# Sign bits of the weights on VectorE or GpSimd, the schedule choosing per piece, in an attention and feed-forward kernel

## The chip, the core and the metric

The kernel runs on one core of a Trainium2 chip. Its engines work side by side, each on its own in-order queue of instructions: TensorE (PE, with weight loads as PEld), VectorE (DVE), ScalarE (ACT), GpSimd (POOL) and SyncE (SP, which here only issues transfers). The metric is the device time of one execution in microseconds, lower is better. A chance or a change is called "faster" or "slower" below only beyond 0.2%.

## The reference

Sliding-window attention with sinks over 4 batches of 8 heads, 768 positions, 64 wide, followed by a feed-forward layer with ELU on the 3072 tokens:

```python
scores = scale * np.matmul(q, k.transpose(0, 1, 3, 2))
keep = is_sink | in_window          # 4 sinks, window 128
a = softmax(np.where(keep, scores, -1e9))
x = (a @ v).transpose(0, 2, 1, 3).reshape(3072, 512)
h = x @ w_in                         # 512 -> 2048
g = np.where(h > 0.0, h, np.exp(np.minimum(h, 0.0)) - 1.0)
out = (g @ w_out).astype(np.float32) # 2048 -> 512
```

The weights `w_in` and `w_out` are 64-bit floats, so each number reaches the chip as two 32-bit words.

## The kernel before

The 24 tiles of 128 tokens are worked in nine chunks of two or three tiles (`SIZES`). A chunk runs through attention (scores, L614 in the first four chunks and L607/L608 later; the masked minimum, L633; the exponential, L635; division and rounding to two 16-bit halves, L685 and L686; a transposing DMA, L704; values, L670 in the first chunk and L718/L723 later) and then through 16 feed-forward steps f. A step is twelve matmuls into `h` (L782), the ELU on ACT, DVE and POOL (L790, L792, L793), rounding to the halves `gh` (L795, ACT) and `gl` (L796, POOL), and matmuls into `acc` (L803). The first two chunks are interleaved: chunk 0 does steps 0 to 6, chunk 1 steps 0 to 12, then both are finished (`PARTS`).

The weights come once, in 32 pieces of 128x512 numbers; piece 2f is for L782 of step f and piece 2f+1 for L803. Piece k is loaded as 128x1024 words into one of six `raw` buffers and rebuilt as a 32-bit float by `weight_f32`: ACT scales the upper word (L308, into a PSUM bank), DVE takes the three top bits of the lower word (L309) and the sign (L310), each into one 16-bit half of the buffer `wu` (two buffers), and DVE joins the three (L311, into `wv`). Then ACT rounds it to 16 bits (L460) and POOL makes the remainder in two halves of 256 columns (L461), both into the tiles `w`. In the rows of the order the tiles `w_135` to `w_166` are pieces 0 to 31, `raw_129` to `raw_134` the six buffers, and `wu_127` and `wu_128` the two.

The order on each queue is not written out. `Plan` is a list scheduler: every task has an engine, a duration, a latency and its dependences; `backward` gives due times from the places of the matmul tasks, `forward` starts the task that is due first among those that are ready, with a lock that makes POOL work and some DVE work (`slow` over 1) exclude each other. A task with `or_` may go to a second engine, whichever picks it first. It is repeated eight times and the best plan is kept (`order`); `keep_order` then emits the instructions in the order of their planned starts. So a change of one task's ways can move any instruction on any queue.

Of the kernel before, what the change touches and what calls it, by code (L numbers as in the profile page):

```python
# [9 lines left out]
F32 = mybir.dt.float32  # L10
F32R = mybir.dt.float32r
F16 = mybir.dt.float16
BF16 = mybir.dt.bfloat16
# [3 lines left out]
ALU = mybir.AluOpType  # L17
# [39 lines left out]
RINGS = dict(tp=2, tp_=2, kqs=2, kq=3, vs=2, vm=1, vt=6, sk=2, e=3, st=6, pq=3, pt=6, g=2, gh=3, x=7, wv=4, s=2, po=1, h=2, wu=2, sv=2, wps=1, raw=6)  # L57
# [44 lines left out]
class Plan:  # L102
# [7 lines left out]
    def add(self, eng, dur, fn, *args, deps=(), lat=0.0, pos=None, or_=None, line=0, slow=1.0, lock=True):  # L110

        t = Task(eng, dur, fn, args, deps, lat, pos, slow)
        t.line = line
        t.lock = lock
        if or_:
            t.ways[or_[0]] = or_[1:]
        self.tasks.append(t)
        return t

    def ring(self, name, writers, users):  # L120

        r = self.rings.setdefault(name, [])
        r.append((writers, users))
# [158 lines left out]
def act_us(n, scaled=False):  # L282
    return 0.17 + 0.00088 * n + (0.08 if scaled else 0.0)
# [6 lines left out]
def pool_us(n):  # L290
    return 0.18 + 0.0019 * n


def dma_us(nbytes):
    return nbytes / 330e3
# [4 lines left out]
def weight_f32(nc, v, d, u, raw):  # L300

    ui = u.bitcast(U16).rearrange("p (f t) -> p f t", t=2)
    words = raw.rearrange("p (f t) -> p f t", t=2)
    halves = raw.bitcast(U16).rearrange("p (f t) -> p f t", t=4)
    return (
        lambda: nc.scalar.activation(d, words[:, :, 1].bitcast(F32), AF.Copy, scale=2.0**-111),  # L308
        lambda: nc.vector.tensor_scalar(ui[:, :, 0], halves[:, :, 1], 13, None, ALU.logical_shift_right),  # L309
        lambda: nc.vector.tensor_scalar(ui[:, :, 1], halves[:, :, 3], 0x8000, None, ALU.bitwise_and),  # L310
        lambda: nc.vector.scalar_tensor_tensor(v.bitcast(I32), d.bitcast(I32), 3, u, ALU.logical_shift_left, ALU.bitwise_or),  # L311
    )
# [49 lines left out]
def fast_path(tc, ctx, first, kq, vx, wt, out, low, spread, numbers, flag):  # L362

    nc = tc.nc
# [4 lines left out]
    def rows(name, shape, dtype, n=None, mem=pool):  # L369
        return [mem.tile(shape, dtype, name=f"{name}{i}") for i in range(n or RINGS[name])]  # L370
# [21 lines left out]
    wu = rows("wu", [P, 512], I32)  # L392
# [18 lines left out]
    add, ring = plan.add, plan.ring  # L411
    turn = {}

    def slot(name):
        turn[name] = turn.get(name, -1) + 1
        return turn[name] % RINGS[name]
# [17 lines left out]
    def weights(k):  # L434
        raw, v = raws[slot("raw")], wv[slot("wv")]

        def load():
            if wide:
                nc.sync.dma_start(raw, wt[k].bitcast(I32))
            else:  # L440
                nc.sync.dma_start(raw[:, :512].bitcast(F32), wt[k])

        def step(i):
            return lambda: weight_f32(nc, v, acc[2], wu[k % RINGS["wu"]], raw)[i]()

        ld = add("SP", 0.4, load, deps=[w_done.get(k - AHEAD, [None])[0]], lat=1.45)
        if wide:
            a = add("ACT", act_us(512), step(0), deps=[ld])
            u1 = add("DVE", 0.446, step(1), deps=[ld], slow=2.0)
            u2 = add("DVE", 0.446, step(2), deps=[ld], slow=2.0)  # L450
            b = add("DVE", 0.7, step(3), deps=[a, u1, u2])
            ring("wu", [u1, u2], [b])
            ring("wps", [a], [b])
            ring("raw", [ld], [a, u1, u2])
            first_acc2.append(b)
        else:
            a = b = add("ACT", act_us(512), lambda: nc.scalar.activation(v, raw[:, :512].bitcast(F32), AF.Copy, scale=W_SCALE), deps=[ld])
            ring("raw", [ld], [a])

        th = add("ACT", act_us(512), lambda: nc.scalar.activation(w[k][:, 0, :], v, AF.Copy), deps=[b])  # L460
        tls = [add("POOL", pool_us(256), lambda c=c: nc.gpsimd.tensor_tensor(w[k][:, 1, c], v[:, c], w[k][:, 0, c], ALU.subtract), deps=[th]) for c in (slice(0, 256), slice(256, 512))]  # L461
        tl = tls[-1]
        ring("wv", [b], tls)
        w_done[k] = th, *tls

    for k in range(NW):
        weights(k)
# [384 lines left out]
    for c, ch in enumerate(CHUNKS):  # L852
        t, n = vm[slot("vm")], len(ch) * P
        src = vx[:, ch[0] * VT : (ch[-1] + 1) * VT].rearrange("p (g w) -> p g w", g=len(ch))
        ld = add("SP", 0.4, lambda t=t, n=n, src=src: nc.sync.dma_start(t.rearrange("p a w -> p (a w)")[:, : NP * n].rearrange("p (g w) -> p g w", w=VT), src), deps=[exps_done[NF * 4 + 8 * c]], lat=dma_us(P * NP * n * 4))
# [293 lines left out]
```

## Time and profile before

| | us |
|---|---|
| median of 3 runs (641.25 to 641.39) | 641.27 |
| the profiled execution, whole | 641.34 |
| its span in the trace | 639.4 |
| PE busy | 613.2 (96%) |
| DVE busy | 424.7 (66%) |
| ACT busy | 423.2 (66%) |
| POOL busy | 361.1 (56%) |

The 1.9 us between the span and the whole lie outside of the trace. The shares of busy time are averages over a start, in which the weights and the first chunks are prepared, and a long stretch after it; they have to be read stretch by stretch. The line numbers are those of the kernel before; behind L452 the changed kernel stands two lines lower, so that its L463 is L461 of before, and its L452 is the new instruction.

### The profile page before, as it was taken

What the parts mean: (1) busy time and instruction counts of PE and PEld (TensorE: products, weight loads), DVE (VectorE), ACT (ScalarE), POOL (GpSimd) and SP (SyncE); (2) the same over time, 40 slices, a digit from 0 to 9 for tenths busy, and PEclk for the clock granted to TensorE, in tenths of its full rate; (3) what the DMA queues carried; (4) which work ended last, traced back from release to release, by engine and by line L of the source; (5) the groups of instructions that cost most, each with busy time, mean ns of one, the idle gap of its engine ahead of it and who ended that gap; (6) DMA issues with size and microseconds to landing.
All of it is one profiled execution on the core that took longest, in us unless ns stands there. A gap on an engine that the chain in (4) does not pass through costs nothing.

```text
span 639.4 us, 13262 instructions
## 1 busy us (share of the span) xinstructions
PE 613.2 (96%) x4475; PEld 366.3 (57%) x4475; DVE 424.7 (66%) x1160; ACT 423.2 (66%) x1216; POOL 361.1 (56%) x630
## 2 busy tenths in 40 slices
PE   5977899999999999999999999999999999999996
PEld 4644565666666555555565655655555556555552
DVE  6998899877666865566666777568567866432222
ACT  5888788877777876676767776677666776432221
POOL 3587799764346766656546667556455664323221
PEclk9978999999999999999999999999999999999999
DMA  8597767467354874365537845446636634210001
GB/s 292 153 315 221 205 254 239 129 178 184 79 121 111 184 156 106 78 206 116 103 96 138 199 100 147 97 159 111 148 76 140 169 87 106 57 45 36 1 2 52
DMA packets 117660, 86.23 MB, mean 135 GB/s; under 512 B 97492, under 2 KB 97492, under 8 KB 117588
## 3 DMA queue, kind: packets, MB, share of 16 engines
q1 hardware_dynamic: 117588, 85.34, 52.3%
q8 instruction: 36, 0.59, 0.4%
q14 instruction: 36, 0.29, 0.2%
HBM read 54.39 MB, written 7.34 MB: 97 GB/s over the span
## 4 chain that ended last, share of the span: by engine, by line
PE 87%; POOL 3%; ACT 3%; DMA 2%; DVE 2%; issue 1%; SPq 0%; POOLq 0%; ACTq 0%; DVEq 0%
PE h L782 38%; PE acc L803 37%; PE po L718 4%; PE s L607 2%; PE s L608 2%; PE s L614 2%; POOL w L461 1%; PE acc L653 1%; DMA kqs<-in_kq_dram 1%; ACT e L635 1%; DMA vs<-in_vx_dram 1%; DMA pt<-pq 1%; ACT pq L685 1%; POOL gl L796 1%; PE po L723 0%
## 5 line engine op out<-in xcount | busy, mean ns | idle before, releaser
L782 PE MATMUL h<-x,w 128*128 128x384 f16 (+1 forms) x1728 | 277.6, 310 | 6.6 <-POOL w L461 3.5
L782 PEld LDWEIGHTS <-w 128*128 128x128 f16 x1728 | 165.2, 98 | 102.9 <-POOL w L461 5.6
L796 POOL TENSOR_TENSOR gl<-g,gh 128x384 f16<-128x384 f32 (+1 forms) x144 | 126.9, 882 | 133.5 <-ACT gh L795 100.1
L803 PE MATMUL acc<-w,gh 128*128 128x512 f16 x768 | 193.2, 381 | 0.0
L790 ACT ACTIVATE g<-h 128x384 f32<-128x384 f32 (+1 forms) x144 | 65.4, 454 | 106.6 <-PE h L782 93.5
L686 DVE SCALAR_TENSOR_TENSOR pq<-e,st,pq 128x256 f16<-128x256 f32 (+1 forms) x176 | 103.2, 618 | 14.4 <-ACT pq L685 14.2
L803 PEld LDWEIGHTS <-gh 128*128 128x128 f16 x768 | 71.0, 98 | 71.6 <-ACT g L790 1.7
L803 PE MATMUL acc<-w,gl 128*128 128x512 f16 x384 | 109.2, 379 | 0.1
L635 ACT ACTIVATE e<-e,st 128x264 f32<-128x264 f32 (+1 forms) x192 | 93.2, 486 | 15.9 <-DVE st L633 14.3
L792 DVE TENSOR_SCALAR g<-g 128x384 f32<-128x384 f32 (+1 forms) x76 | 37.5, 494 | 98.4 <-ACT g L790 98.1
L633 DVE CUSTOM_DVE_ANT_0 e<-s,m 128x264 f32<-128x264 f32 (+1 forms) x192 | 71.6, 404 | 44.1 <-PE s L608 35.9
L795 ACT ACTIVATE gh<-g 128x384 f16<-128x384 f32 (+1 forms) x144 | 69.6, 483 | 34.9 <-DVE g L793 33.2
L685 ACT ACTIVATE pq<-e,st 128x256 f16<-128x256 f32 (+1 forms) x176 | 78.2, 484 | 12.3 <-DVE st L640 6.4
L793 DVE SCALAR_TENSOR_TENSOR g<-g,h 128x384 f32<-128x384 f32 (+1 forms) x144 | 72.6, 504 | 20.0 <-POOL g L792 18.8
L803 PEld LDWEIGHTS <-gl 128*128 128x128 f16 x384 | 37.6, 98 | 45.9 <-POOL gl L796 0.6
L533 POOL TENSOR_TENSOR kq<-kqs,kq 128x528 fp32r<-128x528 f32 (+1 forms) x40 | 49.2, 1231 | 23.6 <-ACT kq L529 23.0
L792 POOL TENSOR_SCALAR g<-g 128x384 f32<-128x384 f32 (+1 forms) x68 | 34.5, 508 | 40.7 <-ACT g L790 34.1
L461 POOL TENSOR_TENSOR w<-wv,w 128x256 f16<-128x256 f32 x64 | 48.5, 774 | 6.2 <-ACT w L460 5.8
L529 ACT ACTIVATE kq<-kqs 128x912 fp32r<-128x912 f32 (+1 forms) x40 | 36.4, 913 | 14.8 <-PE s L608 12.1
L535 POOL TENSOR_TENSOR kq<-kqs,kq 64x384 fp32r<-64x384 f32 x40 | 41.1, 1026 | 3.1
L607 PE MATMUL s<-kq 128*128 128x264 f32 (+1 forms) x120 | 41.3, 365 | 0.0
L718 PE MATMUL po<-pt,vh 128*64 128x128 f16 x656 | 36.4, 223 | 1.7 <-DMA pt<-pq 1.6
(90 smaller groups left out, 642.3 us busy)
## 6 DMA issues: line engine op xcount, KB each, us to landing
raw<-in_wt_dram SPq DMA_DIRECT2D x32, 512.0 KB, 5.3
kqs<-in_kq_dram SPq DMA_DIRECT2D x24, 456.0 KB, 3.9
kqs<-in_kq_dram SPq DMA_DIRECT2D x20, 390.0 KB, 3.4
vs<-in_vx_dram SPq DMA_DIRECT2D x28, 256.0 KB, 3.5
out_dram<-wv SPq DMA_DIRECT2D x24, 256.0 KB, 3.7
vm<-in_vx_dram SPq DMA_DIRECT2D x6, 768.0 KB, 4.7
kqs<-in_kq_dram SPq DMA_DIRECT2D x8, 326.0 KB, 4.2
vm<-in_vx_dram SPq DMA_DIRECT2D x3, 512.0 KB, 4.2
```

The lines of the kernel that those rows point to most:

```text
L633: red = add("DVE", 0.24 + 0.001 * wd, lambda ee=ee, me=me, sp=sps[e], m=m, wd=wd: nc.vector.tensor_tensor_reduce(ee, sp[:, :wd], m[:, :wd] ...
L635: ex = add("ACT", 0.47 + 0.00085 * wd, lambda ee=ee, me=me, rs=rs[:, e : e + 1]: nc.scalar.activation(ee, ee, AF.Exp, bias=me, scale=-1.0, ...
L685: a = add("ACT", act_us(nb * P, True), lambda src=src, hi=hi, re=re: nc.scalar.activation(hi, src, AF.Copy, scale=re), deps=[rr])
L686: b = add("DVE", 0.478 if nb == 2 else 0.33, lambda src=src, hi=hi, lo=lo, re=re: nc.vector.scalar_tensor_tensor(lo, src, re, hi, ALU.mult ...
L718: nc.tensor.matmul(po[e * D : (e + 1) * D, oc], vts[i][x][:, vo : vo + D], pt[:, (2 * e + part) * nb + i, :], start=new, stop=last)
L782: nc.tensor.matmul(hp[:, :n], win[:, part, d, :], xx[:, :n], start=k == 0, stop=k == 3 * ND - 1)
L790: a = add("ACT", act_us(n) + 0.18, lambda gf=gf, hp=hp, sums=sums: nc.scalar.activation(gf, hp[:, :n], AF.Exp, scale=1.0 / G_SCALE, accum_ ...
L792: b = add("DVE", 0.14 + 0.00057 * n, lambda gf=gf: nc.vector.tensor_scalar(gf, gf, -1.0, G_SCALE, ALU.add, ALU.mult), deps=[a], slow=2.1, ...
L793: b = add("DVE", dve_us(n), lambda gf=gf, hp=hp: nc.vector.scalar_tensor_tensor(gf, gf, 0.0, hp[:, :n], ALU.min, ALU.max), deps=[b])
L795: th = add("ACT", act_us(n), lambda gf=gf, gh=gh: nc.scalar.activation(gh[:, :n], gf, AF.Copy), deps=[b])
L796: tl = add("POOL", pool_us(n), lambda gl=gl, gf=gf, gh=gh: nc.gpsimd.tensor_tensor(gl[:, :n], gf, gh[:, :n], ALU.subtract), deps=[th])
L803: nc.tensor.matmul(acc[i], gg[:, i * P : (i + 1) * P], wout[:, part, :], start=f == f0 and k == 0, stop=f == f1 - 1 and k == 2)
```

## The change

In `weights`, the task of the sign bits gets a second way. On DVE it is still L310: a 16-bit AND of the top quarter of the 64-bit number with 0x8000. On POOL it is one `tensor_scalar`: the upper word, read as a 32-bit float with a step of two words, times 0.0, written as bfloat16 into every second 16-bit place; the product is a zero that has the sign of the number, and a bfloat16 zero with sign is the same bits. The task also depends on the task of L309 in the plan. The price that the planner is given for POOL is 0.70 us, against 0.446 us (with `slow` 2.0) on DVE.

```diff
             u1 = add("DVE", 0.446, step(1), deps=[ld], slow=2.0)
-            u2 = add("DVE", 0.446, step(2), deps=[ld], slow=2.0)
+            sign = wu[k % RINGS["wu"]].bitcast(BF16).rearrange("p (f t) -> p f t", t=2)[:, :, 1]
+            high = raw.rearrange("p (f t) -> p f t", t=2)[:, :, 1].bitcast(F32)
+            u2 = add("DVE", 0.446, step(2), deps=[ld, u1], slow=2.0, or_=("POOL", 0.2 + 0.00098 * 512, lambda sign=sign, high=high: nc.gpsimd.tensor_scalar(sign, high, 0.0, None, ALU.mult)))
             b = add("DVE", 0.7, step(3), deps=[a, u1, u2])
```

Of the 32 pieces, 21 have their sign on POOL in the changed kernel: pieces 0 to 10, 12 and 13, and of the last eighteen 15, 16, 21, 24, 26, 28, 29 and 31. Behind that the plan is another one on every engine. Three places follow.

The first is DVE's queue between the masked minima of two tiles of chunk 1 (the tile with `st_98` and the next with `st_99`). Before:

```order
L633 ISA e_95,st_98<-s_170,m_181 128x264
L633 ISA st_98 128x1
L309 TENSOR_SCALAR wu_127<-raw_129 128x512
L310 TENSOR_SCALAR wu_127<-raw_129 128x512
L562 SCALAR_TENSOR_TENSOR vl_85<-vs_64,vh_79 128x512
L311 SCALAR_TENSOR_TENSOR wv_125<-acc_174,wu_127 128x512
L686 SCALAR_TENSOR_TENSOR pq_105<-e_96,st_102,pq_105 128x256 x2
L562 SCALAR_TENSOR_TENSOR vl_86<-vs_63,vh_80 128x512
L633 ISA e_96,st_99<-s_169,m_181 128x264
```

and now:

```order
L635 ISA e_95,st_98<-s_170,m_181 128x264
L635 ISA st_98 128x1
L688 SCALAR_TENSOR_TENSOR pq_105<-e_96,st_102,pq_105 128x256 x2
L564 SCALAR_TENSOR_TENSOR vl_86<-vs_63,vh_80 128x512
L635 ISA e_96,st_99<-s_169,m_181 128x264
```

The piece's three instructions and the first L562 stand earlier in the queue now, and its sign is no longer on DVE.

The second is POOL's queue in chunk 0, around the diagonal products of its tiles (L647, L649 in the new numbering, which PE waits for). Before:

```order
L461 TENSOR_TENSOR w_136<-wv_124,w_136 128x256 x2
L647 TENSOR_TENSOR pq_104<-ident,st_101 128x256
L639 TENSOR_SCALAR st_102<-st_102 128x2
L647 TENSOR_TENSOR pq_105<-ident,st_102 128x256
L647 TENSOR_TENSOR pq_103<-ident,st_97 128x256
L647 TENSOR_TENSOR pq_104<-ident,st_98 128x256
```

and now:

```order
L452 TENSOR_SCALAR wu_127<-raw_133 128x512
L649 TENSOR_TENSOR pq_105<-ident,st_102 128x256
L641 TENSOR_SCALAR st_97<-st_97 128x2
L463 TENSOR_TENSOR w_138<-wv_126,w_138 128x256
L649 TENSOR_TENSOR pq_103<-ident,st_97 128x256
L463 TENSOR_TENSOR w_138<-wv_126,w_138 128x256
L463 TENSOR_TENSOR w_139<-wv_123,w_139 128x256 x2
L649 TENSOR_TENSOR pq_104<-ident,st_98 128x256
L452 TENSOR_SCALAR wu_128<-raw_134 128x512
L452 TENSOR_SCALAR wu_127<-raw_129 128x512
```

Signs and remainders of the weights stand ahead of and between the last three products.

The third is POOL's queue where the remainders of pieces 7 to 10 are made. Before:

```order
L461 TENSOR_TENSOR w_143<-wv_123,w_143 128x256 x2
L692 TENSOR_TENSOR st_97<-e_94,st_97 128x8
L695 CAST pq_103<-st_97 128x2x8
L696 TENSOR_TENSOR pq_103<-st_97,pq_103 128x8
L461 TENSOR_TENSOR w_142<-wv_126,w_142 128x256 x2
L692 TENSOR_TENSOR st_98<-e_95,st_98 128x8
L695 CAST pq_104<-st_98 128x2x8
L696 TENSOR_TENSOR pq_104<-st_98,pq_104 128x8
L461 TENSOR_TENSOR w_144<-wv_124,w_144 128x256 x2
L792 TENSOR_SCALAR g_112<-g_112 128x256
L461 TENSOR_TENSOR w_145<-wv_125,w_145 128x256 x2
```

and now:

```order
L463 TENSOR_TENSOR w_143<-wv_123,w_143 128x256 x2
L452 TENSOR_SCALAR wu_127<-raw_133 128x512
L798 TENSOR_TENSOR gl_119<-g_112,gh_116 128x256
L694 TENSOR_TENSOR st_98<-e_95,st_98 128x8
L697 CAST pq_104<-st_98 128x2x8
L698 TENSOR_TENSOR pq_104<-st_98,pq_104 128x8
L794 TENSOR_SCALAR g_113<-g_113 128x256
L463 TENSOR_TENSOR w_145<-wv_125,w_145 128x256 x2
L463 TENSOR_TENSOR w_142<-wv_126,w_142 128x256 x2
```

Piece 10 (`w_145`, for step 5) went ahead of piece 7 (`w_142`) and of piece 9 (`w_144`).

## Rows read from the trace of the kernel before

**Rows 1.** Stretch after the start: length, busy PE, PEld, DVE, ACT, POOL; granted clock, DMA.
```profile
110.00:480.00 370.00, 370.00 (x2783) 223.13 (x2782) 252.06 (x694) 265.57 (x774) 219.99 (x367) 1.00 0.57 133
```

**Rows 2.** The same view, four stretches of the start.
```profile
14.50:32.00 17.50, 16.48 (x136) 11.68 (x136) 16.55 (x63) 14.29 (x47) 9.62 (x21) 1.00 0.55 169
32.00:48.00 16.00, 11.26 (x64) 6.70 (x64) 14.46 (x40) 13.18 (x40) 13.18 (x24) 0.79 1.03 314
48.00:72.00 24.00, 16.80 (x166) 9.54 (x166) 20.84 (x50) 18.00 (x48) 19.64 (x35) 0.93 0.75 217
72.00:108.65 36.65, 35.78 (x285) 23.31 (x283) 33.95 (x77) 31.07 (x86) 31.58 (x55) 1.00 0.69 222
sum 94.15, PE 80.32 PEld 51.23 DVE 85.80 ACT 76.53 POOL 74.02; mean PE 20.08 PEld 12.81 DVE 21.45 ACT 19.13 POOL 18.51
```

**Rows 3.** Waits of PE from 14.5 to 110 us: total, times, longest.
```profile
PE s L614 <- DVE st L633: 4.2, 2, 3.7
PE h L782 <- POOL w L461: 3.5, 4, 1.1
```

**Rows 4.** Timeline of DVE around PE's longest wait: start, us, instruction.
```profile
37.91 0.47 DVE L310 TENSOR_SCALAR wu<-raw 128x512 uint16<-128x512 uint16 x1
38.28 0.68 DVE L562 SCALAR_TENSOR_TENSOR vl<-vs,vh 128x512 f16<-128x512 f32 x1
...
39.48 1.46 DVE L686 SCALAR_TENSOR_TENSOR pq<-e,st,pq 128x256 f16<-128x256 f32 x2
40.86 0.88 DVE L562 SCALAR_TENSOR_TENSOR vl<-vs,vh 128x512 f16<-128x512 f32 x1
41.66 0.42 DVE L633 CUSTOM_DVE_ANT_0 e<-s,m 128x264 f32<-128x264 f32 x1
```

**Rows 5.** Timeline of PE ahead of that wait and behind it.
```profile
34.85 1.47 PE L782 MATMUL h<-x,w 128*128 128x256 f16 x12 [0.51 <-DVE g L793]
...
42.15 1.60 PE L614 MATMUL s<-kqs 64*128 64x264 f32 x4 [3.74 <-DVE st L633]
43.68 2.74 PE L782 MATMUL h<-x,w 128*128 128x256 f16 x12
```

**Rows 6.** DVE by group, 0 to 72 us: count, busy us, mean ns.
```profile
L310 DVE TENSOR_SCALAR wu<-raw 128x512 uint16<-128x512 uint16 x14 | 9.0, 643 | 0.0
```

**Rows 7.** Line L310, whole run: shortest, median, longest in ns.
```profile
L310 DVE TENSOR_SCALAR wu<-raw x32: 432/542/939, 9.3 to 129.1; 128x512 uint16<-128x512 uint16 x32
```

**Rows 8.** DVE by group, 0 to 140 us: an instruction that both engines run.
```profile
L792 DVE TENSOR_SCALAR g<-g 128x256 f32<-128x256 f32 x10 | 5.5, 549 | 2.0 <-ACT g L790 1.8
```

**Rows 9.** POOL by group, 0 to 140 us.
```profile
L461 POOL TENSOR_TENSOR w<-wv,w 128x256 f16<-128x256 f32 x64 | 48.5, 774 | 6.2 <-ACT w L460 5.8
...
L792 POOL TENSOR_SCALAR g<-g 128x256 f32<-128x256 f32 x19 | 9.9, 520 | 4.8 <-ACT g L790 3.5 <-PE acc L803 1.2
```

**Rows 10.** Line L792 on POOL, 30 to 140 us: shortest, median, longest in ns.
```profile
L792 POOL TENSOR_SCALAR g<-g x19: 400/407/985, 33.9 to 137.6; 128x256 f32<-128x256 f32 x19
```

**Rows 11.** POOL by group, whole run: the same instruction at 384 columns.
```profile
L792 POOL TENSOR_SCALAR g<-g 128x384 f32<-128x384 f32 x40 | 21.0, 525 | 24.1 <-ACT g L790 23.9
```

**Rows 12.** Waits of POOL from 14.5 to 108.65 us: total, times, longest.
```profile
POOL w L461 <- ACT w L460: 3.6, 7, 0.8
...
POOL gl L796 <- ACT gh L795: 2.3, 3, 1.6
POOL g L792 <- ACT g L790: 2.1, 2, 1.6
...
POOL st L639 <- ACT e L635: 1.8, 2, 1.2
POOL g L792 <- PE acc L803: 1.2, 1, 1.2
```

**Rows 13.** Chain that ended last, 40 to 60 us, its longest transfer.
```profile
43.00 5.05 DMA vs<-in_vx_dram
```

**Rows 14.** Timeline of PE: its last wait for a piece of the weights.
```profile
108.69 1.37 PE L782 MATMUL h<-x,w 128*128 128x256 f16 x11 [0.70 <-POOL w L461]
```

## The prediction

> **What bounds the kernel now.** I read the busy time by stretch first, since averages over the whole span say little here. From 110 to 480 us PE is busy all the time [rows 1]: there its own matmuls are the bound, and they are the same after the change. The start is different. From 14.5 to 108.65 us PE is busy 80.3 of 94.15 us, so 13.8 us of it are lost, 4.7 of them between 32 and 48 us and 7.2 between 48 and 72 us [rows 2]. In these two stretches the granted clock falls to 0.79 and 0.93: part of the time PE runs at 1.2 in place of 2.4 GHz behind its waits. The twelve matmuls of one step take 1.47 us ahead of the longest wait and 2.74 us behind it, and the four score matmuls there 1.60 us [rows 5]. So a us of wait that goes at this place can bring more than a us. What is saved in the start is kept, because the long stretch behind it is full; what is not saved there can't come from anywhere else.
>
> Then I read who ends PE's waits there: DVE (the masked minimum L633) 4.2 us, POOL (the remainders L461) 3.5 us [rows 3], and smaller ones by DVE, DMA and ACT. DVE is busy 85.8 of the 94.15 us and POOL 74.0 [rows 2]; DVE is fuller early (16.55 of 17.5 us from 14.5 to 32), POOL late (31.6 of 36.65 us from 72 on). The timeline of DVE shows the longest wait at work. PE waits 3.74 us, until 42.15 us, for the score banks, which a minimum that starts at 41.66 us has to empty; DVE does nothing wrong meanwhile, it works through a sign (L310), two value remainders (L562) and two L686 that stand ahead in its queue [rows 4, 5]. This is a queue that is late as a whole, not one slow instruction.
>
> **What the change takes away.** 21 signs leave DVE, 13 of them among the first 14 pieces, which are all that DVE rebuilds until 72 us. L310 has 0.643 us there on average [rows 6], so 13 x 0.643 = 8.4 us of DVE time go ahead of 72 us. That is the upper end for DVE. Some of it is time that L310 spends blocked, since its shortest run is 0.432 us [rows 7], and that blocking may move to the next DVE instruction; at the shortest duration it is 13 x 0.432 = 5.6 us. DVE's queue thus stands 5.6 to 8.4 us earlier at the end of the start. At the place of the longest wait the plan agrees: between the minima of `st_98` and `st_99` stood a sign, its two neighbours and one more L562, now only two L686 and one L562. By their rows those left take 1.46 + 0.88 us, and the wait of 3.74 us would fall to about 1.5 us from this place alone.
>
> **What it adds.** 21 instructions on POOL. No row shows this one: a 32-bit read with a step of two words and a 16-bit write into every second place. The nearest is L792, also a POOL `tensor_scalar` with one input and two constants: 0.400 us at its shortest with 256 columns [rows 10], 0.525 us on average with 384 [rows 11]. I take 0.51 us as the latter undisturbed (an estimate, just under its mean), so 0.11 us per 128 columns and 0.62 us at 512. In the start L792 takes 0.520 us, 0.12 more than its shortest [rows 9, 10]. I don't add that: it comes from colliding with DVE, and the change takes 21 colliding instructions off DVE. Lower end 0.52 us (the mean at 256 columns, if the narrow write were cheap), upper end 1.55 us (two L461 of 0.774 us, the dearest way in which POOL handles 512 columns of a piece [rows 9]). I stay at 0.62 because one input is nearer to L792 than to L461.
>
> Whether POOL has room is the sum that decides. PE's last wait for a piece ends at 108.69 us, on POOL [rows 14]; up to that piece POOL gets 17 of the 21 signs, and two of them fall ahead of 14.5 us, where POOL is mostly idle. So 15 x 0.62 = 9.3 us have to find room in the 94.15 - 74.0 = 20.1 us that POOL is idle there [rows 2]. Not all of the idle time can be filled: 2.3 + 2.1 + 1.8 us are waits for ACT and 1.2 us for PE [rows 12], 7.4 us in all, which don't hang on DVE. A fuller POOL comes to these waits later, so some of them vanish; I bound the rest by half (3.7) and all (7.4) and take 6.0 us, nearer to all, since ACT's queue gets no work less. The other idle time, like the 3.6 us for L460 [rows 12], which itself waits for DVE's L311, can be filled. Room left for POOL to come earlier: 20.1 - 9.3 - 6.0 = **4.8 us**.
>
> So POOL allows 4.8 us, DVE 5.6 to 8.4 us, and PE has 13.8 us plus the slow clock to give back. The smallest decides: 641.34 - 4.8 = **636.5 us** for the profiled execution, which stands 0.07 us over the median. Its ends with the other terms: 20.1 - 15 x 0.52 - 3.7 = 8.6 us, cut by DVE to 8.4, gives 632.9 us; with 7.4 us left idle the gain is 3.4 us, 637.9 us.
>
> The rest costs nothing by itself. The instruction waits for its transfer and for the L311 that used the same `wu` buffer before; L311 now waits for POOL, and behind it on DVE stand minima and L686, so a late POOL would stop DVE too (second rival). In chunk 0 the last product L647 stands behind two more remainders and a sign than before; PE waits for it, but the plan has put score matmuls ahead of it on PE. Piece 10 goes ahead of pieces 7 and 9 on POOL, two pieces of two L461, 4 x 0.774 = 3.1 us earlier, and PE's step 5 waits for it; this is part of the gain, not more of it.
>
> A rule speaks against the change. L792 runs on both engines in the start, at 256 columns: 0.549 us on DVE and 0.520 us on POOL on average [rows 8, 9], so one-input work is no dearer on POOL there. The Trainium skill's GPSIMD Engine Reference, in section 8 (Key points), calls DVE "structurally ~2× faster" for elementwise work. By it the sign would cost twice the 0.432 us of DVE, 0.86 us, and POOL's room would be 20.1 - 13.0 - 6.0 = 1.1 us: 640.2 us, the next rival. These rows don't agree with the rule, but they show neither the stepped read nor the stepped write.
>
> **Rivals.** *The gain is given back at the next wait*, 640.2 to 642.5 us, say 641.0. For it: PE's waits have several releasers, DVE and POOL alternating [rows 3], DVE's relief ends where a transfer of 5.05 us stands in the chain at 43 us [rows 13], and ACT, busy 13.2 of 16 us, gets weight work earlier ahead of the exponentials. It also comes about at a sign of 0.86 us, by the sum above. Against it: the 4.2 and 3.5 us behind DVE and POOL are over half of what PE loses [rows 2, 3], and the transfers are issued behind DVE's results, so they come earlier with them.
>
> *POOL becomes the bound and the kernel gets slower.* The place is POOL's queue from piece 8 to the last wait at 108.69 us, where it was busy 31.6 of 36.65 us. The room is zero at (20.1 - 6.0) / 15 = 0.94 us a sign. At 1.55 us the room is -9.1 us: 650.5 us; at 1.2 us, as the stepped write might cost, -3.9 us: 645.2 us. It is worse than the sum if L311 holds DVE up behind a late sign. For it: POOL is at 86% in the last stretch already, and no row shows the instruction. Against it: the row nearest to it.
>
> *More than the sum*, 632.9 us or less: POOL's waits for ACT vanish and PE's clock falls in neither stretch [rows 2]. It needs all queues earlier together.
>
> That the change doesn't do what it says is out: 21 signs stand on POOL in the built order.
>
> **How the numbers follow.** Forecast (gain of 2 to 8 us) 0.55; given back 0.21; slower by POOL 0.17; more than the sum 0.07. A measurement tells 0.2% from no change, 640.06 to 642.6 us. Faster than that: 0.55 + 0.07 and a quarter of the given-back case, 0.67; within it 0.15, the rest of that case; slower 0.18, the POOL case and a last bit of the former. The forecast's own range is 633.3 to 639.3 us. The range for 8 in 10 goes on upward over the given-back case and into the slower one: 632.9 to 643.5 us, leaving out about 0.07 below and 0.13 above.
>
> **What would show it.** Right: POOL's `wu` instruction at 0.55 to 0.75 us; no wait of PE for L633 over 2 us near 38 us; PE full before 68 us; PE's waits for L461 no longer in sum; the stretch from 110 us on unchanged in length of work. POOL's idle time up to PE's last wait for a piece falls from 20.1 to about 6 us. Wrong: a sign over 0.94 us, POOL without idle time while PE waits for L461, DVE idle ahead of L311 on POOL, or PE waits that changed their releaser to ACT or DMA with the same sum.

## The result, and the profile after

The changed kernel takes 649.98 us (median of 4 runs, 649.22 to 650.65) against 641.26 us before: ratio 1.0138, 95% interval 1.0121 to 1.0156. It is slower by 8.7 us between the medians, by 8.8 us as the ratio gives it; the forecast was 636.5 us. The profiled execution took 649.22 us with a span of 647.4 us.

Two lines of the page: busy times, and the chain of waits by engine (before: PE 87%, POOL 3%).

```profile
PE 617.5 (95%) x4475; PEld 368.8 (57%) x4475; DVE 422.8 (65%) x1143; ACT 423.5 (65%) x1217; POOL 388.0 (60%) x646
...
PE 85%; POOL 8%; issue 2%; DMA 2%; DVE 1%; ACT 1%; SPq 0%; POOLq 0%; DVEq 0%; ACTq 0%
```

The span grew by 8.0 us. PE's busy time holds 4.3 of them (613.2 before), its idle time 3.7, with the same 4475 matmuls: more of them ran at the lower clock (the mean granted clock is 0.984, before 0.991). POOL grew by 26.9 us, and the new line says why (count, shortest/median/longest in ns, first and last start; then who waited for it):

```profile
L452 POOL TENSOR_SCALAR wu<-raw x21: 1664/1679/1882, 10.6 to 136.5; 128x512 bf16<-128x512 f32 x21
...
  DVE wv L311: 4.2, 5
```

A sign costs 1.68 us on POOL, not 0.62; even its shortest, 1.664 us, is above the prediction's upper end of 1.55. The stretches of the start (columns as in [rows 1]), to be read against [rows 2]:

```profile
14.50:32.00 17.50, 14.21 (x90) 9.85 (x90) 11.87 (x40) 12.05 (x40) 16.70 (x23) 0.80 0.61 200
32.00:48.00 16.00, 13.13 (x84) 8.21 (x84) 12.98 (x47) 12.38 (x38) 14.93 (x27) 0.89 0.77 175
48.00:72.00 24.00, 15.94 (x168) 9.36 (x168) 19.17 (x47) 18.48 (x53) 21.57 (x37) 0.96 0.81 238
72.00:108.65 36.65, 36.65 (x266) 23.30 (x265) 32.26 (x66) 29.18 (x82) 34.07 (x56) 0.93 0.70 216
sum 94.15, PE 79.93 PEld 50.71 DVE 76.27 ACT 72.10 POOL 87.28; mean PE 19.98 PEld 12.68 DVE 19.07 ACT 18.02 POOL 21.82
```

POOL is busy 87.3 of 94.15 us where it was 74.0: 6.9 us of idle time are left of 20.1. DVE fell from 85.8 to 76.3 us. PE finished 608 matmuls where it had finished 651, in nearly the same busy time, at a granted clock of 0.80 in place of 1.00 in the first stretch and 0.93 in place of 1.00 in the last; in the two between it was higher than before.

Yet PE's waits hardly name POOL (14.5 to 110 us: total, times, longest; before: [rows 3]):

```profile
PE s L616 <- DVE st L635: 4.3, 2, 2.6
PE po L720 <- DMA pt<-pq: 3.5, 1, 3.5
PE acc L655 <- POOL pq L649: 2.3, 4, 1.1
```

How POOL gets into them is seen in the chain that ended last, here around 70 us (start, us, what):

```profile
66.50 1.68 POOL wu L452
...
68.20 0.04 DVE wv L311
68.24 0.57 issue
68.81 1.76 DVE pq L688 x2
70.57 0.34 DVE e L635
...
70.93 0.04 issue
70.97 1.93 PE s L616 x4
```

The sign ends, the join L311 that DVE held its queue for can go, two L688 and the masked minimum L635 stand behind it, and PE gets its score banks. PE's wait is put down to DVE, but the chain leads back to POOL's sign. Small POOL instructions behind a sign hold DVE up as well. Ahead of PE's wait of 2.61 us, which ends at 41.83 us, DVE's reciprocal L642 waits for POOL's L641, which stands behind the sign that starts at 36.64 us; that wait is 1.30 us, until 38.63 us. Waits of DVE (0 to 120 us: total, times, longest), 0.4 us in total before:

```profile
DVE st L642 <- POOL st L641: 2.4, 3, 1.3
```

In chunk 0 the way is shorter. Timelines of POOL, and of PE:

```profile
13.77 3.27 POOL L452 TENSOR_SCALAR wu<-raw 128x512 bf16<-128x512 f32 x2
16.97 0.89 POOL L463 TENSOR_TENSOR w<-wv,w 128x256 f16<-128x256 f32 x1
17.81 0.61 POOL L649 TENSOR_TENSOR pq<-ident,st 128x256 f32<-128x256 f32 x1
```

```profile
18.48 0.81 PE L655 MATMUL acc<-pq,e 128*128 128x128 f32 x4 [1.10 <-POOL pq L649]
...
35.78 2.79 PE L784 MATMUL h<-x,w 128*128 128x256 f16 x24
```

Two signs and a remainder stand ahead of the diagonal product that PE waits for. The first feed-forward step starts at 35.78 us; before, it started at 28.53:

```profile
28.53 1.48 PE L782 MATMUL h<-x,w 128*128 128x256 f16 x12
```

Most of that shift is the new plan's own order: in the same plan with all signs on DVE (below) it starts at 33.56 us, and with a quick sign on POOL at 33.95.

### The profile page after: what moved, and what is told of

Its sections match the earlier page's. It is cut to its first block, busy times and chain, and to the rows that moved or that the text cites. A ratio compares the mean times of both kernels' runs of the same rounds, so it can differ in the third digit from the quotient of the medians.

```text
span 647.4 us, 13282 instructions
## 1 busy us (share of the span) xinstructions
PE 617.5 (95%) x4475; PEld 368.8 (57%) x4475; DVE 422.8 (65%) x1143; ACT 423.5 (65%) x1217; POOL 388.0 (60%) x646
## 4 chain that ended last, share of the span: by engine, by line
PE 85%; POOL 8%; issue 2%; DMA 2%; DVE 1%; ACT 1%; SPq 0%; POOLq 0%; DVEq 0%; ACTq 0%
PE h L784 36%; PE acc L805 36%; PE po L720 4%; POOL wu L452 2%; POOL w L463 2%; PE s L609 2%; PE s L616 2%; PE s L610 2%; POOL gl L798 1%; DMA vs<-in_vx_dram 1%; DMA raw<-in_wt_dram 1%; POOL pq L649 1%; PE po L725 0%; PE acc L655 0%; DMA kqs<-in_kq_dram 0%
## 5 line engine op out<-in xcount | busy, mean ns | idle before, releaser
L784 PE MATMUL h<-x,w 128*128 128x384 f16 (+1 forms) x1728 | 277.0, 311 | 1.4 <-DVE g L795 1.2
L784 PEld LDWEIGHTS <-w 128*128 128x128 f16 x1728 | 165.3, 98 | 97.3 <-issue 2.8
L798 POOL TENSOR_TENSOR gl<-g,gh 128x384 f16<-128x384 f32 (+1 forms) x144 | 124.4, 864 | 131.7 <-ACT gh L797 97.8
L792 ACT ACTIVATE g<-h 128x384 f32<-128x384 f32 (+1 forms) x144 | 65.3, 454 | 102.8 <-PE h L784 91.5
L688 DVE SCALAR_TENSOR_TENSOR pq<-e,st,pq 128x256 f16<-128x256 f32 (+1 forms) x176 | 105.0, 628 | 14.6 <-ACT pq L687 14.4
L794 DVE TENSOR_SCALAR g<-g 128x384 f32<-128x384 f32 (+1 forms) x81 | 40.0, 493 | 96.8 <-ACT g L792 96.7
L635 DVE CUSTOM_DVE_ANT_0 e<-s,m 128x264 f32<-128x264 f32 (+1 forms) x192 | 71.3, 405 | 45.8 <-PE s L610 36.5
L794 POOL TENSOR_SCALAR g<-g 128x384 f32<-128x384 f32 (+1 forms) x63 | 30.6, 486 | 36.6 <-ACT g L792 34.1
L463 POOL TENSOR_TENSOR w<-wv,w 128x256 f16<-128x256 f32 x64 | 46.4, 743 | 1.7 <-ACT w L462 1.3
```

The source lines that it names most:

```text
L635: red = add("DVE", 0.24 + 0.001 * wd, lambda ee=ee, me=me, sp=sps[e], m=m, wd=wd: nc.vector.tensor_tensor_reduce(ee, sp[:, :wd], m[:, :wd] ...
L688: b = add("DVE", 0.478 if nb == 2 else 0.33, lambda src=src, hi=hi, lo=lo, re=re: nc.vector.scalar_tensor_tensor(lo, src, re, hi, ALU.mult ...
L784: nc.tensor.matmul(hp[:, :n], win[:, part, d, :], xx[:, :n], start=k == 0, stop=k == 3 * ND - 1)
L792: a = add("ACT", act_us(n) + 0.18, lambda gf=gf, hp=hp, sums=sums: nc.scalar.activation(gf, hp[:, :n], AF.Exp, scale=1.0 / G_SCALE, accum_ ...
L794: b = add("DVE", 0.14 + 0.00057 * n, lambda gf=gf: nc.vector.tensor_scalar(gf, gf, -1.0, G_SCALE, ALU.add, ALU.mult), deps=[a], slow=2.1, ...
L798: tl = add("POOL", pool_us(n), lambda gl=gl, gf=gf, gh=gh: nc.gpsimd.tensor_tensor(gl[:, :n], gf, gh[:, :n], ALU.subtract), deps=[th])
```

## The experiments

**What does the sign's price hang on?** First the form by itself: the kernel before, with a row of POOL instructions behind the end of its work, two of each form:

```diff
+    todo = [(2, "bf", 2, 512), (1, "bf", 2, 512), (2, "bf", 1, 512), (1, "bf", 1, 512), ...]
+        nc.gpsimd.tensor_scalar(dst[t, w][:, :n], src[r][:, :n], 0.0, None, ALU.mult)
+    tasks += forms(nc, raws[0], wv[0], es[0])
```

> The kernel before with 18 more GpSimd instructions behind its last one, on scratch data: the multiplication by 0.0 in seven forms of 512 columns (read with a step of two words or one; written as bfloat16 with a step of two places or one, as float16, as 32-bit float), and the changed kernel's form with 256 and 128 columns, each twice. In the changed kernel the form took 1.68 us. Theory A, the write of every second 16-bit place is dear: forms with that write 1.6 us or more, whatever the read, all others 0.5 to 0.8 us. Theory B, the read with a step of two words is dear: all forms with that read 1.6 us or more. Theory C, bfloat16 is dear: all bfloat16 forms alike, float16 and 32-bit forms 0.5 to 0.8 us. The narrower ones show whether the price goes with the columns: 0.84 us at 256 if it does wholly. The time of the whole kernel is longer by what these instructions add behind the end and says nothing else.

POOL by group behind the end (busy us and mean ns behind the bar; `raw` is read with a step of two words, `wv` word after word). The first group writes with a step, as the sign does, the second without:

```profile
L905 POOL TENSOR_SCALAR e<-raw 128x512 bf16<-128x512 f32 x2 | 3.3, 1662 | 0.1
```

```profile
L905 POOL TENSOR_SCALAR e<-raw 128x512 bf16<-128x512 f32 x2 | 3.0, 1510 | 0.2
```

```profile
L905 POOL TENSOR_SCALAR e<-raw 128x512 f32<-128x512 f32 x2 | 3.0, 1510 | 0.2
L905 POOL TENSOR_SCALAR e<-wv 128x512 f32<-128x512 f32 x2 | 3.0, 1490 | 0.2
...
L905 POOL TENSOR_SCALAR e<-raw 128x256 bf16<-128x256 f32 x2 | 1.9, 931 | 0.2
L905 POOL TENSOR_SCALAR e<-raw 128x128 bf16<-128x128 f32 x2 | 1.1, 571 | 0.2
```

None of the access patterns that the expectation set apart explains it: the plainest form, 32 bits word after word to the same, costs 1.49 us, the stepped read 0.02 more, the stepped narrow write another 0.15, up to 1.66. From 128 to 256 to 512 columns the sign's own form costs 0.57, 0.93 and 1.66 us, some 2.8 to 2.9 ns for a column.

The same question was put in the sign's place. POOL wrote whole words, and the three bits of the lower word came after it, which makes another plan:

```diff
-            u2 = add("DVE", ..., or_=("POOL", ..., lambda ...: nc.gpsimd.tensor_scalar(sign, high, 0.0, None, ALU.mult)))
+            u2 = add("DVE", ..., deps=[ld], ..., or_=("POOL", ..., lambda ...: nc.gpsimd.tensor_scalar(word, high, 0.0, None, ALU.mult)))
+            u1 = add("DVE", 0.446, step(1), deps=[ld, u2], slow=2.0)
```

> As the changed kernel, but GpSimd writes the signed zero as a whole 32-bit float into each word of the buffer, and the VectorE instruction for the low bits comes after it and writes the low half. If the dear part is the bfloat16 write into every second place, the sign takes 0.6 to 0.8 us and the kernel 636 to 641 us. If the read with a step of two words is dear, the sign takes 1.6 us again and the kernel 647 us or more.

Measured 649.96 us, ratio 1.0147 (1.0124 to 1.0170), with 20 signs on POOL; without the stepped write the sign stays dear:

```profile
L451 POOL TENSOR_SCALAR wu<-raw x20: 1513/1695/1967, 9.4 to 136.7; 128x512 f32<-128x512 f32 x20
```

What was left was the operation. The rows that the prediction priced the sign by, L792, are an addition and then a multiplication, two operations; the sign is one. A second row of instructions behind the end:

```diff
+    ops = {"am": (0.0, 0.0, ALU.add, ALU.mult), "mm": (0.0, 1.0, ALU.mult, ALU.mult),
+           "ma": (0.0, 0.0, ALU.mult, ALU.add), "m1": (1.5, None, ALU.mult), "a": (1.5, None, ALU.add)}
```

> As e1, the kernel before with 18 more GpSimd instructions behind its end, all with 512 columns, each twice in a row: plus-then-times on whole 32-bit words, with the stepped read, with the stepped bfloat16 write and with both; times-then-times; times-then-plus; one operation alone with another constant (times 1.5, plus 1.5); a plain copy. If the pair of operations decides: all pairs 0.6 to 0.75 us, the single operations 1.49 us. If only plus-then-times is quick: 0.6 us for those, 1.5 us or more for the other pairs. If the constant 0.0 is what is dear: the singles with 1.5 at 0.6 us. The whole time says nothing else.

Plus then times in its plain form, from the timeline of POOL (start, us):

```profile
631.66 0.62 POOL L909 TENSOR_SCALAR e<-wv 128x512 f32<-128x512 f32 x1
```

Windows of POOL by group: two plain ones with times then times, and one plus then times with the sign's reads and writes; three with times and then times or plus; three with one operation; a copy:

```profile
L909 POOL TENSOR_SCALAR e<-wv 128x512 f32<-128x512 f32 x2 | 1.2, 621 | 0.2
L909 POOL TENSOR_SCALAR e<-raw 128x512 bf16<-128x512 f32 x1 | 0.8, 761 | 0.1
```

```profile
L909 POOL TENSOR_SCALAR e<-wv 128x512 f32<-128x512 f32 x3 | 1.9, 620 | 0.2
```

```profile
L909 POOL TENSOR_SCALAR e<-wv 128x512 f32<-128x512 f32 x3 | 4.5, 1495 | 0.2
```

```profile
L907 POOL COPY e<-wv 128x512 f32<-128x512 f32 x2 | 1.2, 612 | 0.1
```

With two operations, in the three pairs that were run, it is 0.62 us, as much as a copy, and 0.76 us with the sign's stepped write; with one, a times or a plus, 1.49 us. A second operation that does nothing makes the instruction 2.4 times as quick. The Trainium skill's GPSIMD Engine Reference, section 4.1 (Engine selection), calls elementwise work with one input "roughly line-rate" on GpSimd. The forms with two operations stand level with the copy here; the form with one does not.

**The same plan with a cheaper sign.** One operand and one operation more, the order of every queue as in the changed kernel:

```diff
-nc.gpsimd.tensor_scalar(sign, high, 0.0, None, ALU.mult)
+nc.gpsimd.tensor_scalar(sign, high, 0.0, 0.0, ALU.add, ALU.mult)
```

> The changed kernel with the same plan, instruction by instruction; only the GpSimd sign is made by two operations, plus 0.0 and then times 0.0, in place of times 0.0 alone, which gives the same bits. The e1 run showed that read step, write step and type hardly matter (1.49 to 1.68 us), so what is left against L792 (0.40 us at 256 columns) is its pair of operations. If one operation alone is what is dear, the sign takes 0.6 to 0.75 us here, and by the sum of the prediction the kernel takes 634 to 639 us; by the other theory, that the new order of the queues is no better whatever the sign costs (order alone gave a ratio of 1.0014), 640 to 643 us. If the price stays at 1.6 us, 650 us.

Measured 641.03 us, ratio 0.9988 (0.9968 to 1.0009). The sign:

```profile
L452 POOL TENSOR_SCALAR wu<-raw x21: 758/864/1077, 10.3 to 128.0; 128x512 bf16<-128x512 f32 x21
```

The whole loss hangs on the price: from 1.68 to 0.86 us a sign, 1.5% or 9.6 us come back. And at 0.86 us there is no measurable gain.

**Is it the order or the price that the planner was told?** The changed plan with all signs made by DVE:

```diff
-or_=("POOL", 0.2 + 0.00098 * 512, lambda sign=sign, high=high: nc.gpsimd.tensor_scalar(...))
+or_=("POOL", 0.2 + 0.00098 * 512, step(2))
```

> The changed kernel's plan with all 32 sign instructions made by VectorE as before, those 21 at the places in the planned sequence where GpSimd has them. If the price of the sign on GpSimd causes the loss, this is near the time before: 638 to 644 us, with GpSimd as full as before the change. If the new order of all queues is worse by itself, 647 us or more.

642.58 us, ratio 1.0014 (0.9992 to 1.0036): the order alone makes no difference that can be told. PE's waits from 14.5 to 130 us only have other names:

```profile
PE po L718 <- DMA pt<-pq: 7.2, 3, 3.6
PE po L718 <- ACT vh L561: 2.8, 1, 2.8
PE s L614 <- DVE st L633: 1.6, 1, 1.6
```

Then the changed kernel with the true price in the plan:

```diff
-or_=("POOL", 0.2 + 0.00098 * 512, ...
+or_=("POOL", 1.68, ...
```

> The changed kernel, with the plan told that a sign on GpSimd takes 1.68 us in place of 0.70. If only the wrong price misled the plan, the time is 640 to 643 us with fewer signs on GpSimd or at places where it is idle (17 of 32 stay there). If a sign there is a loss whatever the plan knows, since GpSimd is short of time in the start, 644 us or more.

648.61 us, ratio 1.0128 (1.0097 to 1.0159). The planner still gives 17 signs to POOL (1.661 us at the shortest, 1.699 in the middle), and the loss can't be told from that of the changed kernel. A right price in the plan does not mend a dear instruction.

**What is a free sign worth?** The 21 instructions are left out, first in the changed plan, then in the plan before. The two `wu` buffers are set to zero once, so both kernels leave the signs of 21 pieces out of the computation:

```diff
-lambda sign=sign, high=high: nc.gpsimd.tensor_scalar(sign, high, 0.0, None, ALU.mult)
+lambda: None
```

> The changed kernel's own plan, with the 21 instructions on POOL left out and nothing in their place (the two wu buffers are set to zero once at the start; so the signs of 21 pieces are left out of the computation). The sign now costs nothing on either engine: DVE has its relief of 5.6 to 8.4 us and POOL all of its room. The sum of the prediction at a price of zero: POOL 20.1 - 0 - 6.0 = 14.1 us, so DVE decides, 632.9 to 635.7 us. If the gain is given back at waits for transfers and ACT, 638 to 641 us, hardly better than the 641.0 of the sign at 0.86 us: then the price below 0.86 us doesn't matter any more, and no form of the sign on POOL can bring 1%.

638.78 us, ratio 0.9942 (0.9919 to 0.9966).

```diff
-u2 = add("DVE", 0.446, step(2), deps=[ld], slow=2.0)
+u2 = add("DVE", 0.446, (lambda: None) if k in (0, 1, ..., 29, 31) else step(2), deps=[ld], slow=2.0)
```

> The kernel before with its own plan, and the same 21 signs left out of DVE's queue with nothing in their place (wu set to zero once; so the signs of 21 pieces are left out of the computation). POOL gets nothing more. If DVE's queue up to 72 us is what is late, PE gains the 5.6 to 8.4 us of those signs: 632.9 to 635.7 us. If other waits take their place at once, 638 to 641 us. If it is well under the changed plan with the signs left out, that plan's order itself loses; if it is the same, the order is neutral and the relief has one size.

639.41 us, ratio 0.9950 (0.9927 to 0.9973). Both orders agree: with 21 signs off DVE and none on POOL the kernel gains 3.2 to 3.7 us (the intervals reach from 1.7 to 5.2), and a sign on POOL that costs something can hardly bring more in these two plans. Against its own order with all signs on DVE (1.0014) the changed plan gains 4.6 us, which these intervals do not tell from the 3.2 us of the other. PE's waits say where the rest of DVE's relief went; the plan before without the signs, 14.5 to 130 us:

```profile
PE h L784 <- POOL w L463: 5.6, 5, 2.8
PE s L616 <- DVE st L635: 3.6, 2, 3.1
PE po L720 <- DMA pt<-pq: 1.5, 1, 1.5
```

The waits for the remainders on POOL grew from 3.5 to 5.6 us, and the longest wait for a minimum only fell from 3.7 to 3.1 us [rows 3]. In the changed plan the same relief leaves waits for transfers (4.7 us) and ACT's value halves (2.9 us); with all signs on DVE these were 7.2 and 2.8 us.

**Where does the dear sign cost?** The changed plan with one operation for the signs of pieces 0 to 7 and two for the others, and the reverse:

```diff
+... tensor_scalar(sign, high, 0.0, None, ALU.mult) if k < 8 else nc.gpsimd.tensor_scalar(sign, high, 0.0, 0.0, ALU.add, ALU.mult)
```

> The changed kernel's own plan; pieces 0 to 7 keep the sign with one operation (1.68 us), the other 13 signs on POOL get two operations (0.86 us). With two operations everywhere this plan took 0.9988 of before, with one operation everywhere 1.0138. Each half has 8 signs with 0.82 us more, 6.6 us, ahead of PE's last wait for a piece. If the dear sign costs at once in chunk 0, where the diagonal products stand behind it on POOL, and the rest is hidden: 647 to 650 us here, 641 to 643 us in the other run. If it costs where the prediction's rival put it, on POOL from piece 8 on, and the early signs find room: 641 to 643 us here.

> The other half: pieces 0 to 7 with two operations, the 13 signs from piece 8 on with one. By the rival's place (POOL's queue from piece 8 to PE's last wait for a piece) 647 to 650 us, and the run with the dear early signs 641 to 643 us. If the early half is the place, 641 to 643 us here. If POOL's queue is full from the first sign to the last, so that every us of price counts alike wherever it stands, both runs lie half way, 644 to 647 us, and their losses add up to that of the changed kernel.

Early 644.36 us, ratio 1.0040 (1.0025 to 1.0056); late 647.25 us, ratio 1.0076 (1.0048 to 1.0104). Over the 0.9988 of two operations everywhere that is 0.52% and 0.88%, 3.3 and 5.6 us. The eight early signs add 6.6 us in price; the thirteen late ones add 10.7, of which nine, 7.4 us, run ahead of the second mark below. Together the losses make 9.0 us, about the 9.6 us of all signs. Neither half is the place by itself; of the cases expected, the third one for the late run, with losses that add up, comes nearest. PE's order is the same in the five kernels of this plan, so two of its waits mark the way (the 350th or 351st and the 666th to 668th recorded matmul; timelines of PE). In turn: the 21 signs left out, two operations, late dear, early dear, all dear:

```profile
62.26 0.30 PE L722 MATMUL po<-pt,vh 128*64 128x128 f16 x4 [2.61 <-DMA pt<-pq]
...
105.22 0.30 PE L722 MATMUL po<-pt,vh 128*64 128x128 f16 x4 [1.19 <-DMA pt<-pq]
```

```profile
64.14 0.43 PE L720 MATMUL po<-pt,vh 128*64 128x128 f16 x4 [3.35 <-DMA pt<-pq]
...
107.60 0.30 PE L720 MATMUL po<-pt,vh 128*64 128x128 f16 x4 [1.10 <-DMA pt<-pq]
```

```profile
65.67 0.42 PE L720 MATMUL po<-pt,vh 128*64 128x128 f16 x4 [3.46 <-DMA pt<-pq]
...
111.98 0.30 PE L720 MATMUL po<-pt,vh 128*64 128x128 f16 x4 [1.95 <-DMA pt<-pq]
```

```profile
67.64 0.42 PE L720 MATMUL po<-pt,vh 128*64 128x128 f16 x4 [3.42 <-DMA pt<-pq]
...
111.05 0.30 PE L720 MATMUL po<-pt,vh 128*64 128x128 f16 x4 [1.12 <-DMA pt<-pq]
```

```profile
68.69 0.30 PE L720 MATMUL po<-pt,vh 128*64 128x128 f16 x4 [3.50 <-DMA pt<-pq]
...
114.50 0.30 PE L720 MATMUL po<-pt,vh 128*64 128x128 f16 x4 [1.84 <-DMA pt<-pq]
```

Against two operations, the early dear signs are 3.5 us late at the first mark and still 3.5 at the second; the late ones are 1.5 and 4.4 us late, all of them 4.6 and 6.9. From the second mark to the end of the span it is 531.2 to 533.7 us in all five. The span with all signs dear is 7.9 us longer than with two operations, and 6.9 of them are there at the second mark; of the late ones' 6.2 us it is 4.4. Only the sign's form on POOL differs between these runs, so most of the loss arises from it by 115 us, in both halves, and it is kept.

**The better form, planned for.** Two operations with the price 0.86 us told:

```diff
-or_=("POOL", 0.2 + 0.00098 * 512, ... (sign, high, 0.0, None, ALU.mult)
+or_=("POOL", 0.86, ... (sign, high, 0.0, 0.0, ALU.add, ALU.mult)
```

> The changed kernel with the sign as plus 0.0, then times 0.0 (0.86 us measured in its place), and the planner told 0.86 us in place of 0.70. The plan is another one: 22 signs on POOL. If the planner lost time because it believed a wrong price, the plan made with the true one gains over the same form under the old plan (641.0): 637 to 640 us. If what is gained on DVE is given back at the next wait whatever the plan says, it stays at 640 to 642 us.

And two operations on whole words, with the three bits after them as above, told 0.75 us:

```diff
-or_=("POOL", 0.2 + 0.00098 * 512, ... (sign, high, 0.0, None, ALU.mult)
+or_=("POOL", 0.75, ... (word, high, 0.0, 0.0, ALU.add, ALU.mult)
```

> The sign on POOL as plus 0.0, then times 0.0, written as whole 32-bit words (no stepped write; the three top bits of the lower word then come after it on DVE), with the planner told 0.75 us: 23 signs on POOL. By the instruction alone 0.64 us, in its place perhaps 0.7 to 0.8. By the sum of the prediction 15 x 0.75 leaves POOL 2.9 us: 638.4 us; if the gain is given back at the next wait, 640 to 642 us.

640.56 us, ratio 0.9967 (0.9944 to 0.9990), and 639.77 us, ratio 0.9965 (0.9944 to 0.9987): both a little faster than the kernel before, by about 2 us, and not to be told from each other. The traces have 18 and 25 signs on POOL, where the expectations say 22 and 23. The second one's sign:

```profile
L451 POOL TENSOR_SCALAR wu<-raw x25: 639/659/1088, 9.4 to 127.4; 128x512 f32<-128x512 f32 x25
```

## Why the prediction was wrong, point by point

**The step that failed: the price of the sign**, "I stay at 0.62 because one input is nearer to L792 than to L461". L792 has the engine, the instruction and the single input in common with the sign, and the estimate of 0.62 us for 512 columns was right for its form: 0.62 us is what the forms with two operations took. But L792 has two constants, as the prediction says itself, and so two operations; the sign has one, which no row of before showed on POOL, and that costs 1.49 us by itself and 1.66 with the stepped write. The upper end of 1.55 us, two L461, was no bound either.

**POOL's room** was the limit, as the sum had it. With the measured price the prediction's own sum gives 20.1 - 15 x 1.68 - 6.0 = -11.1 us, 652.4 us; measured was a loss of 8.8 us. With 0.86 us it gives 640.2 us; measured was 0.9988, 640.6 us of the profiled 641.34. The threshold of 0.94 us lies between the two; a straight line between the two measured ratios crosses 1 at 0.93 us (an estimate; with the first ratio's interval about 0.8 to 1.0). From 0.86 to 1.68 us a us more in price cost 0.78 us of time where the sum has 1: 9.6 us, where 15 x 0.82 = 12.3 us were added. From a sign left out to one of 0.86 us it cost only 0.23: 2.9 us, where 15 x 0.86 = 12.9 us were added. So there is room on POOL, and it is used up near the price that the sum gave. The idle time that can't be filled was put at 6.0 us, and 6.9 us are left in the changed kernel; that stretch holds less of the work now (608 matmuls, before 651), so how near these two figures are is partly luck.

**The rival "POOL becomes the bound"** is what happened, at 1.68 us 650 us where it had 650.5 us at 1.55. Its place was too narrow: not only from piece 8 on, where 5.6 us arose, but from the first eight signs as well, 3.3 us. With these eight dear, PE's waits for POOL's products L649 are 2.2 us, where two operations have 0.7, and those for the minimum L635 are 2.7 us, where two operations have 1.4. The prediction had let the products go with the score matmuls ahead of them on PE. They did not cover it: in the changed kernel PE waited 2.3 us there.

**DVE's relief** was over-sized, a second failure that the first one hides. 5.6 to 8.4 us less on DVE's queue are worth 3.2 to 3.7 us of time against the kernel before (signs left out, either plan), so the forecast's gain of 4.8 us was more than a free sign brought; the interval of 1.7 to 5.2 us does not shut it out. With a sign of 0.66 us, near the assumed one, and a plan of its own the gain was 2.2 us (0.9965). The rest is the rival "given back": POOL's remainders, transfers and ACT come next. At the place of the longest wait the number came out and its reason did not. The wait was to fall "to about 1.5 us", and with a sign of 0.86 us it is 1.45 us. But with all signs on DVE, in the same order, it is 1.63 us, with a sign (L310) still between the two minima. So nearly all of the fall there is the new order's. Timelines of PE, two operations and all signs on DVE:

```profile
38.84 1.06 PE L616 MATMUL s<-kqs 64*128 64x264 f32 x4 [1.45 <-DVE st L635]
```

```profile
38.63 1.06 PE L614 MATMUL s<-kqs 64*128 64x264 f32 x4 [1.63 <-DVE st L633]
```

**The lower clock** made the loss larger, as the prediction had it for gains: over half of the 8.0 us of span are busy time. Twelve L784 take 2.74 us behind a wait at 72.83 us, and 1.48 us at 78.72 us.

**The marks** given for "wrong" were seen in part: a sign over 0.94 us, and DVE held ahead of L311 by POOL (4.2 us). Others did not tell the cases apart. POOL's idle time fell to 6.9 us and PE's waits for L463 were gone, which the prediction had given as marks for "right"; the waits of PE stood behind other instructions.

## What to carry to other kernels

Price a new instruction by a row that has the same operation count, not only the same engine, shape and inputs; where there is none, take a run of that form by itself first, behind the end of the kernel. Where an engine's queue is the narrow place, set the room against the count times the price and look at the price at which it is used up: here the two prices measured in one order lay on the sides of it that the sum had given, although the forecast was wrong. And a relief on one queue is worth at most what the next queue allows; leaving the work out on both sides measures that limit directly.

## What the hardware showed that was not expected

On GpSimd a `tensor_scalar` with one operation takes 1.49 us for 128x512 32-bit floats, with two operations 0.62 us, and a copy 0.61 us. With one operation that held for a times and a plus with 32-bit results, and for a times with 16-bit results; it grows by the column (0.57, 0.93, 1.66 us for 128, 256, 512 columns in the sign's form). A write into every second 16-bit place adds 0.12 to 0.15 us at 512 columns, a read with a step of two words 0.02 us. Why one operation is the dearer form no run here shows.
